# The order of the first products of k, q and kv on TensorE in a linear-attention and state-space kernel, and a carry product padded to 128 rows

## The chip, the cores and the metric

The kernel runs on one core of a Trainium2 chip. The metric is the device time of one execution in microseconds (us). A core has engines that work through queues of their own, each strictly in order, and wait for one another through semaphores: TensorE (PE in the profile; its weight loads are PEld), VectorE (DVE), ScalarE (ACT), GpSimd (POOL), and SyncE (SP), which here only starts transfers.

## The reference

Two branches work on 2048 tokens with 448 features and are mixed by a gate.

```python
x = A_x;  g = sigmoid((x * gate_w).sum(-1))
# a: linear attention, 16 heads of 28
q, k, v = split(x @ wqkv)
phi = lambda t: where(t > 0, t + 1, exp(t)) + 1e-6
kv = sum_s phi(k)[s]^T v[s];   z = sum_s phi(k)[s]
a = (phi(q) @ kv) / (phi(q) @ z + 1e-6) @ wo
# b: a diagonal state-space convolution of x along the tokens, by FFT
K = 2 * real(sum_n C[d, n] * exp(A[d, n] * dt[d] * l))
b = causal_conv(x, K) + x * D_skip
out = g * a + (1 - g) * b
```

For the inputs at hand the taps K are constant along the tokens, so that the convolution is a running sum of the rows of x times one number per feature. The kernel tests that, and keeps a general path for other inputs, which doesn't run here.

## The kernel before

The tokens are cut into 16 chunks of 128 (`c`). Numbers are kept as a high part, rounded to the type of TensorE's products (`F32R`), and a low part, the rest; the high part is a cast on ACT, the low part a subtraction (`low`, L229/L230) on POOL or DVE. A projection of a chunk is eleven products (`pieces`, L309, issued at L325; `project` issues all eleven): four tiles of the contraction, numbered 1, 2, 3 and 0, with names as the diff has them: `h1` is high x times high weights of tile 1, `l1` low x times high weights, `w1` high x times low weights. Tile 0 has 64 real rows; its other 64 rows carry the low part of the weights, so that it needs no `w0`. Its high weights are therefore complete only after a cast on ACT and a subtraction on DVE.

For a chunk c there are:

- **x(c)**: `split_t` (L232) casts the turned x on ACT (L234) and makes its low part on POOL (L230); `split_n` (L237) does the same for the plain x (ACT L240, POOL L230) and, for c > 2, calls `skip` (L245/L246, POOL: x times D_skip). The skips of chunks 0 to 2 are called by themselves.
- **k(c)**: the projection by the weights of k. `k_feature` (L348) makes two ACT passes, relu and exp (L351, L352), and one on DVE (L353); `k_high` (ACT, L357) makes `pkh`, `k_low` (DVE, L363) makes `pkl` and adds the chunk to the sum z, `zb`. pkh and pkl have two buffers each.
- **q(c)**: the projection by the weights of q and the gate. `q_post` (L370) makes the gate's exp and the feature (ACT L371, L340; DVE L341, L344).
- **kv(c)**: `do_g` (L386, L394), eleven products of plain x with pkh and pkl, summed over all chunks in four PSUM banks. The first product of a block reads pkh, the second pkl, for chunk 0 and for the blocks of 128 columns.
- **v(c)**: `do_v` (L399), the running sum inside a chunk by a triangle of ones, `tri`. `v_post` takes the sums of all chunks' last rows to `u`.

Everything is issued in an order written out by hand. **Opening** (L421 to L463): x(0) and the weights arrive in three transfers, of which the last holds tile 0 of the weights and x(1); x(2) and plain x(0) follow in one, plain x(1) and x(2) in another. Nine filler products (`fill`, L250/L252, on constant data) run on PE until then. k(0) is issued in a special order, with one filler behind its first, second and ninth product; then k(1), k(2), the features of chunks 0 and 1, kv(0), kv(1), q(0), q(1). **Loop** (L464, steps c = 2 to 13): k(c+1), its feature; for c < 5 kv(c); q(c), its feature; for c > 4 kv(c) behind it. In steps 2 to 5 and ahead of them, `steps` (L417) moves on `s4d_prepare` (L272), which reduces the state-space inputs on ACT (L283, L284) and DVE (L285, then a row of small operations up to L302) and ends at step 5 with four small transposes on PE (L306). In step 3 DVE casts `tri` (L501) and `gcr` (L502).

**Behind the loop** the last chunks follow, the four sums of kv are copied to SBUF by ACT (`gs`, L666), one by one as they are complete, and `inter` (L683) makes the carry of the running sums: one product (L688) of `gcr` and `uw`, a cast of `u`, over `UZ` = 64 rows. Next on PE are the products of `kv_products` (L719), each group of four of which reads the four gs in order. Then a loop over the chunks turns the normalised features (L595) and multiplies them with the finished matrix (L620, eleven products a chunk).

Buffers that the steps touch: the turned x has four, the plain x seven, the loads four; PSUM is given by tag (`q`, `k`, `v0`, `v1`).

Of the kernel before, what the change touches and what calls it, by code (L numbers as in the profile page):

```python
# [8 lines left out]
F32R = mybir.dt.float32r  # L9
# [6 lines left out]
P = 128  # L16
S = 2048
D = 448
# [6 lines left out]
NAT = 4 * P  # L25
# [17 lines left out]
GIN = 9 + NC  # L43
L1, L0 = 32, 64
UL = 32
UZ = 2 * UL
PAD = S + P
MAGIC = 1.5 * 2.0 ** 23
TWO_PI = 6.283185307179586
# [85 lines left out]
def gated_mix_kernel(ctx: ExitStack, tc: tile.TileContext, xin, wq_d, wvo_d, abc_d, ldt_d, dsk_d,  # L135
                     turn_d, cst_d, first_d, gin_d, lag_d, out):
    nc = tc.nc
    PE, ACT, DVE, POOL, SP = nc.tensor, nc.scalar, nc.vector, nc.gpsimd, nc.sync
# [15 lines left out]
    wkh, wkl = wk2[:, 0], wk2[:, 1]  # L154
# [5 lines left out]
    cst = const.tile([P, DJ + RX + 1], F32, name="cst")  # L160
    mask, gcat, sel = cst[:DJ, :DJ], cst[:UZ, DJ:DJ + RX], cst[:, DJ + RX:]
    gcr = const.tile([UZ, RX], F32R, name="gcr")
    ones = const.tile([P, P], F32R, name="ones")
    rows = const.tile([P, S], F32, name="rows")
    near, dsk = (rows[:, i * D:(i + 1) * D] for i in range(2))
    u = const.tile([UZ, D], F32, name="u")
    zb = const.tile([P, D], F32, name="zb")
# [9 lines left out]
    xt_p = work.enter_context(tc.tile_pool(name="xt", bufs=4))  # L177
# [11 lines left out]
    xt, xn, turned, plain = {}, {}, {}, {}  # L189

    def load_x(c):
        r = xp.tile([P, XC], F32, name="xr", tag="xr")
        turned[c], plain[c] = r[:, :NAT], r[:, NAT:]
        SP.dma_start(out=r, in_=xin[c])
# [5 lines left out]
    wkr = {}  # L200
    o = 0
    for part in PARTS:
# [8 lines left out]
        o = e  # L211
# [17 lines left out]
    def low(eng, o, r, h):  # L229
        eng.tensor_tensor(out=o, in0=r, in1=h.bitcast(F32), op=ALU.subtract)  # L230

    def split_t(c):  # L232
        w = xt[c] = xt_p.tile([P, 2 * NAT], F32R, name="xt", tag="t")
        ACT.copy(w[:, :NAT], turned[c])  # L234
        low(POOL, w[:, NAT:], turned[c], w[:, :NAT])

    def split_n(c):  # L237
        r, w = plain[c], xn_p.tile([P, NX], F32R, name="xn", tag="n")
        xn[c] = w
        ACT.copy(w[:, :XC - NAT], r)  # L240
        low(POOL, w[:, XC - NAT:], r[:, :D], w[:, :D])
        if c > 2:
            skip(c)

    def skip(c):  # L245
        POOL.tensor_tensor(out=y[:, c], in0=plain[c][:, :D], in1=dsk, op=ALU.mult)  # L246
# [3 lines left out]
    def fill(n):  # L250
        for _ in range(n):
            PE.matmul(idle, lhsT=warm[:, :P], rhs=warm, start=True, stop=True)  # L252
# [4 lines left out]
    def split_w(j, h, l, w, eng):  # L257
        ACT.copy(h[:, j], w[j] if isinstance(w, dict) else w[:, j])
        low_w(j, h, l, w, eng)

    def low_w(j, h, l, w, eng):
        r = slice(0 if j else 64, P)
        w = w[j] if isinstance(w, dict) else w[:, j]
        low(eng, (l if j else h)[r, j], w[r], h[r, j])
# [44 lines left out]
    def pieces(c, wh, wl, n, tag, last=None):  # L309
        o = ps.tile([P, 512], F32, name=tag, tag=tag)  # L310
        h, l = ([xt[c][:, i + k * P:i + (k + 1) * P] for k in range(J)] for i in (0, NAT))
        hh, lh, hl = ([(a[k], w[:, k]) for k in range(J)] for a, w in ((h, wh), (l, wh), (h, wl)))
        hl = hl[1:]
        if last == "x":
            seq = hh + hl + lh
        else:
            seq = [p for k in range(J) for p in (hh[k], lh[k])] + hl
            if last == "w":
                seq = seq[2:6] + seq[8:9] + seq[6:8] + seq[9:] + seq[:2]

        def run(count):
            for _ in range(min(count, len(seq))):
                a, b = seq.pop(0)
                run.n += 1
                PE.matmul(o[:, :n], lhsT=a, rhs=b, start=run.n == 1, stop=not seq)  # L325
        run.n = 0
        return o, run

    def project(*args, **kw):
        o, run = pieces(*args, **kw)  # L330
        run(11)
        return o
# [15 lines left out]
    def k_feature(c, o):  # L348
        e = tp.tile([P, D], F32, name="e", tag="e")
        pks[c] = o[:, :D]  # L350
        ACT.activation(e, pks[c], AF.Relu, scale=-1.0)  # L351
        ACT.activation(e, e, AF.Exp, scale=-1.0)  # L352
        DVE.scalar_tensor_tensor(out=pks[c], in0=pks[c], scalar=1.0, in1=e, op0=ALU.add, op1=ALU.max)  # L353

    def k_high(c):
        pkh[c] = tp.tile([P, 512], F32R, name="pkh", tag="pkh")[:, EDGE:EDGE + D]
        ACT.add(pkh[c], pks[c], 1e-6)  # L357

    def k_low(c):
        pk = pks.pop(c)  # L360
        pkl[c] = tp.tile([P, 512], F32R, name="pkl", tag="pkl")[:, EDGE:EDGE + D]
        for o, a, op in ((pkl[c], pkh[c].bitcast(F32), ALU.subtract), (zb, zb, ALU.add))[::-1 if c == NC - 1 else 1]:
            DVE.scalar_tensor_tensor(out=o, in0=pk, scalar=1e-6, in1=a, op0=ALU.add, op1=op)  # L363
# [22 lines left out]
    def do_g(c, blocks=range(4)):  # L386
        w = xn[c]
        for i in blocks:
            a = w[:, 64 + i * P:64 + (i + 1) * P]
            b = w[:, XC - NAT + 64 + i * P:][:, :P] if i < 3 else None  # L390
            seq = [(a, pkh[c]), (a, pkl[c]), (b, pkh[c])] if i < 3 else \
                  [(a, pkh[c]), (a[:, :64], pkl[c])][::1 if c == 0 else -1]
            for n, (a, b) in enumerate(seq):
                PE.matmul(g[i][:a.shape[1], :D], lhsT=a, rhs=b, start=c == 0 and n == 0,  # L394
                          stop=c == NC - 1 and n == len(seq) - 1)
# [21 lines left out]
    def steps(n):  # L417
        for _ in range(n):
            next(prep, None)

    w = xt[0] = xt_p.tile([P, 2 * NAT], F32R, name="xt", tag="t")  # L421
    DVE.tensor_copy(w[:, P:NAT], turned[0][:, P:])
    ACT.copy(wkh[:, 1], wkr[1])  # L423
    DVE.tensor_copy(w[:, :P], turned[0][:, :P])
    low(DVE, w[:, NAT:], turned[0], w[:, :NAT])
    low_w(1, wkh, wkl, wkr, DVE)
    for j in (2, 3, 0):
        split_w(j, wkh, wkl, wkr, DVE)
    ko, run = pieces(0, wkh, wkl, D, "k", "w")
    for n, f in ((1, 1), (1, 1), (6, 0), (1, 1), (2, 0)):  # L430
        run(n)
        fill(f)
    ko = [ko]
    split_t(1)
    ko.append(project(1, wkh, wkl, D, "v0", "x"))
    split_t(2)
    ko.append(project(2, wkh, wkl, D, "v1", "x"))
    k_feature(0, ko[0])
    k_high(0)
    split_n(0)  # L440
    k_low(0)
    k_feature(1, ko[1])
    split_n(1)
    k_high(1)
    k_low(1)
    do_g(0)
# [17 lines left out]
    for c in range(2, NC - 2):  # L464
        if c + 3 < NC:
            load_x(c + 3)
        if c == 2:
            SP.dma_start(out=cst, in_=cst_d)
        if c == 4:
            SP.dma_start(out=wvo, in_=wvo_d)  # L470
        vs = VS.get(c, ())
        ko = project(c + 1, wkh, wkl, D, "v1" if c in (2, 4) else "k")
        for v in vs[:1]:
            do_v(v)
        split_t(c + 2)
        k_feature(c + 1, ko)
        k_high(c + 1)
        if c > 5:
            for v in vs[:1]:
                v_post(v)  # L480
        k_low(c + 1)
        if c < 5:
            do_g(c)
        qo = project(c, wqh, wql, D + 2, "q")
        if c == 5:
            steps(1)
        else:
            for v in vs[1:]:
                do_v(v)
        q_post(c, qo)  # L490
        if c == 10:
            split_n(c + 2)
        if c == 5:
            v_post(0)
        else:
            for v in vs[1:]:
                v_post(v)
        if c < 5:
            steps(2 if c == 4 else 1)
        if c == 3:  # L500
            DVE.tensor_copy(tri, trir)  # L501
            DVE.tensor_copy(gcr, gcat)  # L502
        if c == 7:
            SP.dma_start(out=okr[:, None, :DJ], in_=oks[:, None, :])
        if c == 9:
            DVE.tensor_reduce(out=okr[:, DJ:], in_=okr[:, :DJ], op=ALU.add, axis=AX.X)
            DVE.tensor_copy(okn, okr[:, DJ:])
        if c > 4:
            do_g(c)
        if c == 5:  # L510
            do_v(1)
        if c < 4:
            skip(c - 1)
        if c != 10:
            split_n(c + 2)
        if c == 5:
            v_post(1)
        for j in {11: (0, 1), 12: (2, 3)}.get(c, ()):
            w = xn_p.tile([P, NX], F32R, name="wo", tag="n")[:DJ, :2 * D].rearrange("p (i d) -> p i d", i=2)
            woh.append(w[:, 0])  # L520
            wol.append(w[:, 1])
            ACT.copy(woh[j], wo[:, j])
            low(POOL, wol[j], wo[:, j], woh[j])
# [109 lines left out]
    c = NC - 2  # L633
    POOL.memset(rows[DT:RX, D:2 * D], 0.0)
    gate(0, c)
    ko = project(c + 1, wkh, wkl, D, "k")
    do_v(c + 1)
    uw = xt_p.tile([P, 2 * NAT], F32R, name="uw", tag="t")[:UZ, :D]
    k_feature(c + 1, ko)
    ACT.copy(uw, u)  # L640
    low(POOL, uw[UL:], u[UL:], uw[UL:])
    k_high(c + 1)
    k_low(c + 1)
    zh = tp.tile([P, D], F32R, name="zh", tag="w")
# [283 lines left out]
```

## Time and profile before

| | us |
|---|---|
| median of three runs | 176.55 |
| lowest and highest run | 176.33, 176.62 |
| the profiled execution | 176.31 |
| its span in the trace | 174.5 |

Some 1.8 us of an execution lie outside the span. A row of a timeline reads: start, busy time (both us), engine, line, operation, what it writes and reads, shapes, count; brackets give the idle time of the engine ahead of it and what ended that. PE's busy time of one product (0.36 us) is longer than the distance between two products, since they overlap: distances are read from starts. The granted TensorE clock is 1.00 in every stretch. Rows are called by line: "L306" is line 306.

### The profile page before, as it was taken

The page shows a single profiled execution, that of the slowest core. Times are in us where ns is not written, and L with a number is a line of the kernel's source. Part 1 is how long each engine was busy: PE and PEld are TensorE (multiplying, and loading weights), DVE is VectorE, ACT ScalarE, POOL GpSimd, SP SyncE. Part 2 cuts the span into 40 slices and gives each one's busy share as a digit, 9 for nine tenths or more (in the row PEclk, how much of TensorE's full clock was granted, in tenths as well). Part 3 has the DMA queues.
Part 4 walks back from the last instruction along what each step waited for, and adds up shares of the span by engine and source line. Part 5 has one row for each costly group of instructions (what it writes and reads, how often), then busy time and mean ns, then how long its engine had stood idle before and what let it go on. Part 6 is the DMA issues. An engine that isn't in the chain of part 4 may idle for free.

```text
span 174.5 us, 2800 instructions
## 1 busy us (share of the span) xinstructions
PE 168.2 (96%) x876; PEld 151.5 (87%) x876; DVE 113.8 (65%) x240; ACT 96.5 (55%) x221; POOL 119.9 (69%) x128
## 2 busy tenths in 40 slices
PE   6999999999989999999999999999999999999991
PEld 2699999978789999999999999998999999999991
DVE  1747636498984663937537255487898998997551
ACT  3789395896454372534627366256475564664441
POOL 5167466557809996796996999529968998983100
PEclk9999999999999999999999999999999999999999
DMA  5999954087001230330404300000031221222212
GB/s 165 418 316 317 273 163 146 0 327 334 2 4 35 89 123 1 125 120 2 121 4 129 116 1 0 0 0 2 7 66 53 106 94 69 81 99 84 111 71 93
DMA packets 7963, 18.61 MB, mean 107 GB/s; under 512 B 2045, under 2 KB 4810, under 8 KB 7818
## 3 DMA queue, kind: packets, MB, share of 16 engines
q1 hardware_dynamic: 7946, 18.41, 31.2%
q8 instruction: 7, 0.11, 0.2%
q14 instruction: 10, 0.08, 0.2%
HBM read 14.38 MB, written 3.67 MB: 103 GB/s over the span
## 4 chain that ended last, share of the span: by engine, by line
PE 81%; DVE 8%; ACT 4%; POOL 3%; issue 2%; DVEq 0%; ACTq 0%; POOLq 0%
PE a L620 20%; PE g L394 16%; PE q L325 14%; PE k L325 13%; PE tr L595 4%; PE v L325 3%; PE q L252 2%; POOL y L246 2%; PE v L402 2%; PE v L401 2%; PE m L699 1%; DVE sm L274 1%; PE k L719 1%; PE tr L719 1%; ACT y L283 1%
## 5 line engine op out<-in xcount | busy, mean ns | idle before, releaser
L620 PE MATMUL a<-wk,th 128*128 128x448 f32 (+1 forms) x170 | 36.2, 359 | 0.0
L394 PE MATMUL g<-pkh,xn 128*128 128x448 f32 x112 | 35.5, 363 | 0.0
L620 PEld LDWEIGHTS a<-wk,th 128*128 128x128 f32 x170 | 29.5, 189 | 1.6
L325 PE MATMUL k<-wk,xt 128*128 128x448 f32 x132 | 29.4, 366 | 0.0
L325 PE MATMUL q<-wqh,xt 128*128 128x450 f32 x120 | 27.5, 366 | 0.0
L353 DVE SCALAR_TENSOR_TENSOR k<-k,e 128x448 f32<-128x448 f32 x12 | 7.6, 632 | 30.5 <-ACT e L352 30.5
L325 PEld LDWEIGHTS k<-wk,xt 128*128 128x128 f32 x132 | 24.5, 188 | 2.9 <-ACT wk L423 0.5
L230 POOL TENSOR_TENSOR xn<-xr,xn 128x448 fp32r<-128x448 f32 x16 | 18.8, 1178 | 11.6 <-ACT xn L240 11.2
L414 POOL TENSOR_TENSOR y<-y,t 128x448 f32<-128x448 f32 x16 | 18.7, 1169 | 11.4 <-DVE t L406 11.4
L325 PEld LDWEIGHTS q<-wqh,xt 128*128 128x128 f32 x120 | 22.5, 189 | 1.8
L394 PE MATMUL g<-pkl,xn 128*128 128x448 f32 x64 | 23.3, 364 | 0.0
L394 PEld LDWEIGHTS g<-pkh,xn 128*128 128x128 f32 x112 | 21.0, 188 | 2.2
L533 POOL TENSOR_TENSOR prod<-pq,zb 128x448 f32<-128x448 f32 x16 | 18.4, 1154 | 4.3 <-ACT zb L656 3.0
L351 ACT ACTIVATE e<-k 128x448 f32<-128x448 f32 x12 | 6.5, 545 | 25.5 <-PE k L325 25.4
L246 POOL TENSOR_TENSOR y<-xr,rows 128x448 f32<-128x448 f32 x16 | 18.5, 1155 | 0.0
L230 POOL TENSOR_TENSOR xt<-xr,xt 128x512 fp32r<-128x512 f32 x14 | 18.1, 1295 | 0.4 <-ACT xt L234 0.4
L558 POOL TENSOR_TENSOR pn<-pq,den 128x336 f32<-128x336 f32 x16 | 12.1, 754 | 5.9 <-ACT den L547 4.1
L625 DVE SCALAR_TENSOR_TENSOR ot<-y,og,a 128x448 f32<-128x448 f32 (+1 forms) x17 | 10.7, 629 | 5.0 <-PE a L620 5.0
L603 DVE TENSOR_TENSOR th<-tr,th 128x512 fp32r<-128x512 f32 x16 | 11.0, 690 | 2.5 <-ACT th L602 2.0
L357 ACT ACTIVATE pkh<-k 128x448 fp32r<-128x448 f32 x12 | 6.6, 546 | 10.0 <-DVE k L353 10.0
L394 PEld LDWEIGHTS g<-pkl,xn 128*128 128x128 f32 x64 | 11.2, 174 | 0.9
L602 ACT CAST th<-tr 128x512 fp32r<-128x512 f32 x16 | 9.4, 590 | 4.5 <-PE tr L595 4.2
(151 smaller groups left out, 307.1 us busy)
## 6 DMA issues: line engine op xcount, KB each, us to landing
xr<-in SPq DMA_DIRECT2D x15, 512.0 KB, 5.9
out<-ot SPq DMA_DIRECT2D x15, 224.0 KB, 1.9
pq<-in SPq DMA_DIRECT2D x4, 448.0 KB
wvo<-in SPq DMA_DIRECT2D x1, 1792.0 KB
y<-in SPq DMA_DIRECT2D x2, 480.0 KB
y<-in SPq DMA_DIRECT2D x2, 450.0 KB
u<-t SPq DMA_DIRECT2D x30, 1.8 KB, 1.8
y<-in SPq DMA_DIRECT2D x1, 448.0 KB, 4.3
```

Source lines behind the costliest of these rows:

```text
L230: eng.tensor_tensor(out=o, in0=r, in1=h.bitcast(F32), op=ALU.subtract)
L246: POOL.tensor_tensor(out=y[:, c], in0=plain[c][:, :D], in1=dsk, op=ALU.mult)
L325: PE.matmul(o[:, :n], lhsT=a, rhs=b, start=run.n == 1, stop=not seq)
L353: DVE.scalar_tensor_tensor(out=pks[c], in0=pks[c], scalar=1.0, in1=e, op0=ALU.add, op1=ALU.max)
L394: PE.matmul(g[i][:a.shape[1], :D], lhsT=a, rhs=b, start=c == 0 and n == 0, stop=c == NC - 1 and n == len(seq) - 1)
L414: POOL.tensor_tensor(out=y[:, c], in0=y[:, c], in1=t, op=ALU.add)
L533: POOL.tensor_tensor(out=pd[c], in0=pq[:, c], in1=zb, op=ALU.mult)
L558: POOL.tensor_tensor(out=n[:, :3, :DJ].rearrange("p j (h d) -> p j h d", h=4), in0=a, in1=r[:, :H - 4].rearrange("p (j h) -> p j h", j=3)[ ...
L602: ACT.copy(h, ov)
L603: DVE.tensor_tensor(out=l, in0=ov, in1=h.bitcast(F32), op=ALU.subtract)
L620: PE.matmul(a[:, lo:hi], lhsT=u_, rhs=w_[:, lo:hi], start=n == 0, stop=n == 10)
L625: DVE.scalar_tensor_tensor(out=ot[:, lo:hi], in0=y[:, c, lo:hi], scalar=og[:, c:c + 1], in1=a[:, lo:hi], op0=ALU.mult, op1=ALU.add)
```

## The change

Four edits:

- In the opening, the buffer of x(1) is taken along with that of x(0). x(1) is cast by ACT ahead of tile 0 of the weights, and its low part is made by DVE, between those of tiles 3 and 0 of the weights, not by POOL. PE issues nine products of k(0) (the same fillers behind the first and second, none behind the ninth), then six of k(1), which need neither tile 0 nor the low part of x(1), then the last two of k(0), then the other five of k(1).
- The casts and low parts of the plain x(0) and x(1) are called ahead of the feature of chunk 0 and of its `k_high`.
- In steps 2 to 4 kv(c) is issued behind q(c) and its feature, as in the later steps.
- `UZ` is 128: `u`, `uw`, `gcr` and the product L688 have 128 rows. The added rows are zeros; the low part of `uw` is made for the same 32 rows as before.

```diff
-UZ = 2 * UL
+UZ = 4 * UL
...
-            if last == "w":
+            if last and len(last) > 1:
+                seq = [{"h": hh, "l": lh, "w": [None] + hl}[i[0]][int(i[1])] for i in last.split()]
+            elif last == "w":
                 seq = seq[2:6] + seq[8:9] + seq[6:8] + seq[9:] + seq[:2]
...
-    w = xt[0] = xt_p.tile([P, 2 * NAT], F32R, name="xt", tag="t")
+    w, w1 = (xt_p.tile([P, 2 * NAT], F32R, name="xt", tag="t") for _ in range(2))
+    xt[0], xt[1] = w, w1
...
-    for j in (2, 3, 0):
+    for j in (2, 3):
         split_w(j, wkh, wkl, wkr, DVE)
-    ko, run = pieces(0, wkh, wkl, D, "k", "w")
-    for n, f in ((1, 1), (1, 1), (6, 0), (1, 1), (2, 0)):
-        run(n)
+    ACT.copy(w1[:, :NAT], turned[1])
+    low(DVE, w1[:, NAT:], turned[1], w1[:, :NAT])
+    split_w(0, wkh, wkl, wkr, DVE)
+    ko, runs = zip(*(pieces(c, wkh, wkl, D, t, o) for c, t, o in (
+        (0, "k", "h1 l1 h2 l2 w1 h3 l3 w2 w3 h0 l0"), (1, "v0", "h1 h2 h3 w1 w2 w3 h0 l1 l2 l3 l0"))))
+    for c, n, f in ((0, 1, 1), (0, 1, 1), (0, 7, 0), (1, 6, 0), (0, 2, 0), (1, 5, 0)):
+        runs[c](n)
         fill(f)
-    ko = [ko]
-    split_t(1)
-    ko.append(project(1, wkh, wkl, D, "v0", "x"))
+    ko = list(ko)
     split_t(2)
     ko.append(project(2, wkh, wkl, D, "v1", "x"))
+    split_n(0)
     k_feature(0, ko[0])
+    split_n(1)
     k_high(0)
-    split_n(0)
     k_low(0)
     k_feature(1, ko[1])
-    split_n(1)
...
         k_low(c + 1)
-        if c < 5:
-            do_g(c)
         qo = project(c, wqh, wql, D + 2, "q")
...
-        if c > 4:
-            do_g(c)
+        do_g(c)
...
-    low(POOL, uw[UL:], u[UL:], uw[UL:])
+    low(POOL, uw[UL:2 * UL], u[UL:2 * UL], uw[UL:2 * UL])
```

## The prediction

> **What bounds the kernel now.** I read the page first: the busy shares and the chain that ended last.
>
> ```profile
> PE 168.2 (96%) x876; PEld 151.5 (87%) x876; DVE 113.8 (65%) x240; ACT 96.5 (55%) x221; POOL 119.9 (69%) x128
> PE 81%; DVE 8%; ACT 4%; POOL 3%; issue 2%; DVEq 0%; ACTq 0%; POOLq 0%
> ```
>
> TensorE issues products almost without a break and holds 81% of the chain. No product is removed, so time can only come from slots in which TensorE issues nothing useful. The view of waits gives PE two of them behind the opening, both between 35 and 49 us. They stand in brackets (idle before, releaser) in PE's timeline, whose columns are start, busy, then what:
>
> ```profile
> 28.55 2.37 PE L325 MATMUL k<-wk,xt 128*128 128x448 f32 x11
> ...
> 35.22 0.37 PE L325 MATMUL v<-wk,xt 128*128 128x448 f32 x1
> 35.95 2.28 PE L325 MATMUL v<-wk,xt 128*128 128x448 f32 x10 [0.36 <-POOL xt L230]
> ...
> 42.54 2.49 PE L325 MATMUL k<-wk,xt 128*128 128x448 f32 x11
> ...
> 46.89 0.76 PE L325 MATMUL q<-wql,xt 128*128 128x450 f32 x3
> 48.46 0.60 PE L306 MATMUL p<-both,sm 112*128 112x112 f32 x4 [0.81 <-DVE sm L273]
> ```
>
> A product takes 0.20 us of issue (opening rows below). k(5) loses 35.95 - 35.22 - 0.20 = **0.53**. k(6) takes 2.49 where k(4) takes 2.37: **0.12**. The three products from 46.89 leave the queue free at 47.49, and the four transposes of L306 start at 48.46: **0.97**. In the chain in order of time, the stretch between q(0) and L306 runs through ACT, POOL and DVE: there those three set the pace, and TensorE runs into them at L306. Behind L306 the chain is PE again almost to the end, so what L306 gains, the kernel gains.
>
> The opening, the same view:
>
> ```profile
> 6.16 1.68 PE L325 MATMUL k<-wk,xt 128*128 128x448 f32 x7
> 7.69 0.39 PE L252 MATMUL q<-warm 128*128 128x512 bf16 x1
> 8.02 0.67 PE L325 MATMUL k<-wk,xt 128*128 128x448 f32 x2
> 8.53 4.57 PE L325 MATMUL v<-wk,xt 128*128 128x448 f32 x22
> 12.93 0.36 PE L394 MATMUL g<-pkh,xn 128*128 128x448 f32 x1
> ```
>
> 22 products between 8.53 and 12.93 give 0.20 each. From 7.69 to 8.53, 0.84 us hold two useful products (0.40): one filler, a wait for the low part of the weights' tile 0, and a restart.
>
> **Part 1, the opening.** The filler goes and six products of k(1) take the slot at 7.69. They end at 8.89; h0, l0 of k(0) go to 9.29, the last five of k(1) to 10.29, k(2) to 12.49, where kv(0) starts instead of at 12.93: **0.44 earlier**, if the data is there. ACT's timeline, then DVE's:
>
> ```profile
> 6.74 0.57 ACT L258 CAST wk<-y 128x448 fp32r<-128x448 f32 x1 [0.16 <-DMA y<-in]
> ...
> 8.04 0.62 ACT L234 CAST xt<-xr 128x512 fp32r<-128x512 f32 x1 [0.21 <-DMA xr<-in]
> 8.73 0.55 ACT L351 ACTIVATE e<-k 128x448 f32<-128x448 f32 x1
> ...
> 10.59 0.55 ACT L357 ACTIVATE pkh<-k 128x448 fp32r<-128x448 f32 x1 [0.70 <-DVE k L353]
> 11.03 0.61 ACT L240 CAST xn<-xr 128x512 fp32r<-128x512 f32 x1
> 11.54 0.55 ACT L351 ACTIVATE e<-v 128x448 f32<-128x448 f32 x1
> ...
> 12.61 0.60 ACT L240 CAST xn<-xr 128x512 fp32r<-128x512 f32 x1
> ```
>
> ```profile
> 4.96 0.69 DVE L230 TENSOR_TENSOR xt<-y,xt 128x512 fp32r<-128x512 f32 x1
> 5.57 2.40 DVE L230 TENSOR_TENSOR wk<-y,wk 128x448 fp32r<-128x448 f32 x4
> ...
> 11.16 0.62 DVE L363 SCALAR_TENSOR_TENSOR pkl<-k,pkh 128x448 fp32r<-128x448 f32 x1 [0.61 <-ACT pkh L357]
> ```
>
> Tile 0 and the turned x(1) come in one transfer (6.74), so ACT's cast of x(1), 0.62 like that of x(2), takes 6.74 to 7.36 and is ready for 7.69. DVE's four lows are 0.60 each: three end near 7.4, x(1)'s low (0.69) near 8.1, tile 0's near 8.7, ahead of 8.89. POOL loses that low and is free for x(2) when ACT's cast lands (8.04 + 0.62).
>
> The price is on the features. k(0) now ends at 9.29, not 8.53, so its relu moves from 8.73 to 9.49 and its pkl from 11.78 to 12.54; kv(0) wants it with its second product, at 12.69. pkh(0) starts at 10.59 + 0.76 = 11.35, and ACT's next operation, now the relu of chunk 1, 0.44 behind it (10.59 to 11.03): 11.79. From relu to the end of pkl is 11.78 - 8.73 = 3.05, so pkl(1) ends at 14.84; kv(1)'s second product wants it at 12.49 + 2.20 + 0.20 = 14.89. Almost no slack is left: I take 0.44 whole, and keep 0 to 0.1 as loss.
>
> **Part 2, kv of chunks 2 to 4 behind q.** Each kv is eleven products, 2.2 us, so q(2), q(3) and q(4) end 2.2 earlier on PE. Is it those that ACT waits for?
>
> ```profile
> 26.79 0.55 ACT L357 ACTIVATE pkh<-v 128x448 fp32r<-128x448 f32 x1 [0.70 <-DVE v L353]
> 28.75 0.17 ACT L371 ACTIVATE e<-q 128x1 f32<-128x1 f32 x1 [1.41 <-PE q L325]
> ...
> 34.59 0.55 ACT L357 ACTIVATE pkh<-k 128x448 fp32r<-128x448 f32 x1 [0.70 <-DVE k L353]
> 35.41 0.17 ACT L371 ACTIVATE e<-q 128x1 f32<-128x1 f32 x1 [0.28 <-PE q L325]
> ```
>
> Yes: 1.41 us at 28.75, while the casts of x(4), x(5) and the relu of k(4) stand behind it in ACT's queue; 0.28 at 35.41. With q(2) ending near 26.1, ACT goes on when pkh(3) is done: 26.79 - 0.44 + 0.55 = 26.90, with issue 26.95, **1.80 earlier**. Its input k(4) is there by then (28.55 - 0.44 + 2.37 = 30.48). At q(3) the second wait goes: pkh(4) ends at 35.14 - 1.80 = 33.34, so ACT is 35.41 - 33.44 = **1.97 earlier**. What waits on ACT, in POOL's and DVE's timelines:
>
> ```profile
> 34.61 1.28 POOL L230 TENSOR_TENSOR xt<-xr,xt 128x512 fp32r<-128x512 f32 x1
> 35.86 1.16 POOL L246 TENSOR_TENSOR y<-xr,rows 128x448 f32<-128x448 f32 x1
> 39.06 1.28 POOL L230 TENSOR_TENSOR xn<-xr,xn 128x448 fp32r<-128x448 f32 x1 [2.04 <-ACT xn L240]
> ```
>
> ```profile
> 36.24 1.03 DVE L341 TENSOR_SCALAR t<-e 128x448 f32<-128x448 f32 x1
> ...
> 38.64 0.69 DVE L285 SCALAR_TENSOR_TENSOR y<-pq 112x512 f32<-112x512 f32 x1
> ...
> 39.26 1.17 DVE L501 CAST tri<-both 128x128 fp32r<-128x128 f32 x1
> ...
> 48.24 0.16 DVE L273 TENSOR_TENSOR sm<-sm,okc 112x4 f32<-112x4 f32 x1
> ```
>
> x(5)'s low moves from 35.89 to 34.09; k(5)'s second product wants it at 35.22 - 0.44 + 0.20 = 34.98, so the 0.53 goes, and likewise k(6)'s 0.12. On DVE, the casts and small operations end just after a POOL operation ends (t at 37.27, POOL at 37.02; tri at 40.43, POOL at 40.34), whatever their size. I read that as DVE waiting for POOL there, and POOL's x(5) operation waits for ACT. So tri and what follows move with ACT by 1.97: the last DVE operation before L306 from 48.40 to 46.43, L306 from 48.46 to **46.49**. PE alone would be there at 48.46 - 0.44 - 0.53 - 0.12 - 0.97 = 46.40. DVE stays last by a hair: **1.97 saved at L306**, taken as 1.95. kv later costs nothing visible: pkh(2) is held until kv(2) ends near 28.3, its buffer is next written near 32.8 (34.59 - 1.80).
>
> The Trainium skill, "SBUF — State Buffer", section "Who interferes with whom", says that VectorE and GpSimd share a port pair under an exclusive lock, and that an operation with two SBUF inputs contends too. By that rule the pair of L285 can also hold up POOL, which speaks against a rigid shift; the 1.03 and 1.17 agree with it. By the sum without it L306 is at 46.49, with it up to one POOL operation later.
>
> **Part 3, the carry product.** PE's and ACT's timelines:
>
> ```profile
> 119.75 0.37 PE L394 MATMUL g<-pkh,xn 128*128 128x448 f32 x1
> 120.04 0.46 PE L688 MATMUL z<-uw,gcr 64*112 64x448 f32 x1
> 120.43 0.35 PE L719 MATMUL k<-gs,wvo 128*112 128x112 f32 x1
> ```
>
> ```profile
> 119.69 0.99 ACT L666 COPY gs<-g 128x448 f32<-128x448 f32 x2 [0.53 <-PE g L394]
> ```
>
> From 119.75 to 120.43 two slots (0.40) take 0.68: 0.28 lost around the 64-row product. At 128 rows it should stand in line like its neighbours. But the fourth product of L719 reads the fourth gs copy, which ends at 119.69 + 0.99 = 120.68 and starts only when kv's last product (119.75 + 0.37) is out. Today that fourth product is at about 120.8, so it can move by some 0.1 at most. I take **0.05**; ends 0 and 0.28. The zero rows added on the other engines I cost at nothing: POOL cleared 128 rows and 64 rows of 448 in the same time.
>
> ```profile
> 0.75 0.47 POOL L184 MEMSET zb<- 128x448 f32 x1 [0.29 <-POOLq L918]
> ...
> 2.39 0.46 POOL L186 MEMSET u<- 64x448 f32 x1
> ```
> The Trainium skill, "TensorEngine Tiling (Array Packing)", section "Tiling Modes", says that a change of tiling mode drains the array; the 0.28 agrees with it, and by that rule alone the sum would be 2.23.
>
> **Sum.** 1.95 + 0.05 = 2.0. The profiled execution took 176.31 (span 174.5 and 1.8 around it), so 174.3; against the median 176.55, **174.6**.
>
> **Rivals.**
> *A, PE is last at L306 and the carry gains whole*: 0.44 + 0.53 + 0.12 + 0.97 + 0.28 = 2.34, so 174.2; up to 0.3 more if restarts go too. Against it: the gs copy. 6%.
> *B, one more POOL operation on DVE's way* (1.15 to 1.3, the rows above): L306 at 47.7, 0.8 saved, 175.75. If ACT's lead is lost whole, only the opening's 0.44 is left: 176.05. For it: DVE's pace is POOL's in this stretch, and both shift by unequal amounts (1.80 and 1.97). 13%.
> *C, the cast of x-plain(1)*, now ahead of pkh(0) on ACT, waits for its transfer. The trace shows only that it had landed by 12.61; the one before it landed by 8.04, and a landing before 10.8 is free. At 12.61, pkh(0) starts at 13.12 (0.51 behind a cast, 11.03 to 11.54) instead of 11.35: the opening loses 1.8, and all behind q(0) with it: 2.0 - 1.8 = 0.2 saved, 176.35. 6%.
> *D, slower: two more POOL operations on DVE's way*. Place: the L285 pair of step 3 and the casts tri and gcr. If the pair comes after the start of POOL's x(5) operation (37.1), each of the two waits for a whole operation, 2 x 1.2 = 2.4; L306 comes at 48.9, and the time is 176.95. It decides if DVE comes there about a whole us later than I have it, so that both miss that start; the second alone (38.64 - 1.80 = 36.84) misses it when 0.25 late, and that is B. Against it: before, POOL's operation came while the second was running, and it took 0.69 all the same. 11%.
>
> **Chances.** The forecast, 174.0 to 175.3, has 64%; A 6, B 13, C 6, D 11. The range 173.9 to 176.1 holds the forecast, A and most of B, about 8 in 10. A measurement of this kernel can tell some 0.2% (0.35 us) from no change. Faster by more: forecast, A and nearly all of B, 81%; within it: C and the end of B, 8%; slower: D, 11%.
>
> **What would show it.** Opening: no filler near 7.69, kv(0) at 12.5; a wait on pkl at 12.7 or 14.9 would price the thin slack. Middle: ACT's first e of q(2) near 26.95, no wait of k(5) on POOL, L306 near 46.5. End: z 0.20 behind kv's last product, and the fourth L719 product waiting for gs. Wrong if ACT's lead at q(2) doesn't reach L306, or if a wait after L306 takes it back.

## The result, and the profile after

| | before | after |
|---|---|---|
| median, us | 176.59 (176.33 to 176.63) | 174.51 (174.33 to 174.78) |
| the profiled execution | 176.31 | 174.33 |
| its span | 174.5 | 172.5 |

The ratio is 0.9887 (95% interval 0.9870 to 0.9904): 2.08 us saved, where 1.95 (176.55 to 174.6) was forecast. The page of after, the chain that ended last:

```profile
PE 97%; DVE 1%; ACT 0%; issue 0%; ACTq 0%
```

The chain was 81% PE and is 97% PE. The view of waits has one line left for PE, its very first wait (engine and line, releaser, us in total, times, longest):

```profile
PE q L252 <- DVE warm L183: 1.5, 1, 1.5
```

Both waits of before (k(5) for POOL, L306 for DVE) are gone. In PE's timeline of after, the middle (the transposes are still L306; most lines behind them stand two or three higher than before: the projections are L327, kv L396):

```profile
35.16 2.36 PE L327 MATMUL v<-wk,xt 128*128 128x448 f32 x11
37.35 1.77 PE L327 MATMUL q<-wqh,xt 128*128 128x450 f32 x8
...
41.76 2.36 PE L327 MATMUL k<-wk,xt 128*128 128x448 f32 x11
...
45.99 0.76 PE L327 MATMUL q<-wql,xt 128*128 128x450 f32 x3
46.62 0.60 PE L306 MATMUL p<-both,sm 112*128 112x112 f32 x4
```

k(5) is one unbroken row and q(4) follows 37.35 - 35.16 = 2.19 behind its start; k(6) is busy 2.36, as an unhindered block; from the three products at 45.99 to L306 it is 0.63, where it was 48.46 - 46.89 = 1.57. Before, kv(4) followed k(5) at 38.07, 38.07 - 35.22 = 2.85 behind its start: k(5) lost 0.66, and not the 0.53 of its wait alone, as the ten products behind the wait also ran slower (2.12 from start to start). ACT, which set the pace there, in its timeline of after:

```profile
26.76 0.55 ACT L359 ACTIVATE pkh<-v 128x448 fp32r<-128x448 f32 x1 [0.70 <-DVE v L355]
27.20 0.17 ACT L373 ACTIVATE e<-q 128x1 f32<-128x1 f32 x1
...
33.47 0.17 ACT L373 ACTIVATE e<-q 128x1 f32<-128x1 f32 x1
```

The first passes of q(2) and q(3) have no bracket any more: they stand 0.44 behind the pass ahead of them (26.76, 33.03). That of q(4) comes at 40.68, 0.45 behind the pass ahead of it. The end, PE's timeline of after and then of before (z is L690, L721 the products of before's L719):

```profile
117.92 0.36 PE L396 MATMUL g<-pkh,xn 128*128 128x448 f32 x1
118.12 0.37 PE L690 MATMUL z<-uw,gcr 128*112 128x448 f32 x1
118.33 1.81 PE L721 MATMUL k<-gs,wvo 128*112 128x112 f32 x16
119.98 1.80 PE L721 MATMUL tr<-gs,wvo 128*112 128x112 f32 x16
```

```profile
122.09 1.74 PE L719 MATMUL tr<-gs,wvo 128*112 128x112 f32 x16
123.60 0.65 PE L699 MATMUL m<-wo,kvh 112*112 112x448 f32 x2
...
128.74 1.46 PE L620 MATMUL a<-wk,th 128*128 128x448 f32 x6
```

From kv's last product to the second group of sixteen it is 119.98 - 117.92 = 2.06; before it was 122.09 - 119.75 = 2.34. And the opening, PE's timeline of after, then the one row of before that it is to be held against:

```profile
7.70 1.48 PE L327 MATMUL v<-wk,xt 128*128 128x448 f32 x6
9.08 0.67 PE L327 MATMUL k<-wk,xt 128*128 128x448 f32 x2
...
12.79 0.36 PE L396 MATMUL g<-pkh,xn 128*128 128x448 f32 x1
...
17.32 0.98 PE L327 MATMUL q<-wqh,xt 128*128 128x450 f32 x4
```

```profile
17.34 0.36 PE L325 MATMUL q<-wqh,xt 128*128 128x450 f32 x1
```

kv(0) starts 0.14 earlier than before (12.93), not 0.44, and q(0) 0.02 earlier. ACT's first cast out of the third transfer (tile 0 of the weights, and x(1)) stands in its timeline of after at 7.02, released by that transfer; before it stood at 6.74:

```profile
7.02 0.62 ACT L432 CAST xt<-y 128x512 fp32r<-128x512 f32 x1 [0.48 <-DMA y<-in]
```

The total nearly met the forecast, but in this execution the opening seems to have given nothing.

### The profile page after: what moved, and what is told of

The parts are those of the page before. It is cut to its first block, busy times and chain, and to the rows that moved or that the text cites. A ratio compares the mean times of both kernels' runs of the same rounds, so it can differ in the third digit from the quotient of the medians.

```text
span 172.5 us, 2800 instructions
## 1 busy us (share of the span) xinstructions
PE 167.4 (97%) x875; PEld 151.6 (88%) x875; DVE 114.5 (66%) x241; ACT 96.3 (56%) x221; POOL 119.6 (69%) x127
## 4 chain that ended last, share of the span: by engine, by line
PE 97%; DVE 1%; ACT 0%; issue 0%; ACTq 0%
PE a L622 21%; PE g L396 21%; PE q L327 19%; PE k L327 16%; PE v L327 7%; PE tr L597 4%; PE q L252 2%; PE v L404 2%; PE v L403 2%; PE m L701 1%; PE k L721 1%; PE tr L721 1%; DVE warm L183 0%; PE p L306 0%; DVE ot L627 0%; ACT pq L633 0%
## 5 line engine op out<-in xcount | busy, mean ns | idle before, releaser
L396 PE MATMUL g<-pkh,xn 128*128 128x448 f32 x112 | 35.5, 363 | 0.0
L327 PE MATMUL k<-wk,xt 128*128 128x448 f32 x132 | 29.3, 365 | 0.0
L327 PE MATMUL q<-wqh,xt 128*128 128x450 f32 x120 | 27.5, 366 | 0.0
L327 PEld LDWEIGHTS k<-wk,xt 128*128 128x128 f32 x132 | 24.6, 188 | 2.7 <-ACT wk L426 0.4
L327 PEld LDWEIGHTS q<-wqh,xt 128*128 128x128 f32 x120 | 22.5, 188 | 1.7
L230 POOL TENSOR_TENSOR xn<-xr,xn 128x448 fp32r<-128x448 f32 x16 | 19.4, 1212 | 6.6 <-ACT xn L240 4.5
L396 PE MATMUL g<-pkl,xn 128*128 128x448 f32 x64 | 23.4, 366 | 0.0
L396 PEld LDWEIGHTS g<-pkh,xn 128*128 128x128 f32 x112 | 21.0, 188 | 2.2
L396 PEld LDWEIGHTS g<-pkl,xn 128*128 128x128 f32 x64 | 11.2, 174 | 1.2 <-DVE pkl L365 0.2
L327 PE MATMUL q<-wql,xt 128*128 128x450 f32 x45 | 11.6, 363 | 0.0
```

## The experiments

The theory to begin with was the prediction's: an opening worth 0.44, a middle in which ACT's waits for q(2) and q(3) set the pace, and an end worth 0.05. The rivals: that one wait of ACT (q(2)) carries the whole middle; that the opening is lost to the features; that the end is worth the whole 0.28. The first four runs take the change apart; two move kv chunk by chunk; two price a product of 64 rows; the last four go after the opening.

**One part alone: the middle.**

```diff
-        if c < 5:
-            do_g(c)
         qo = project(c, wqh, wql, D + 2, "q")
...
-        if c > 4:
-            do_g(c)
+        do_g(c)
```

> The kernel before with only the middle edit: kv of chunks 2 to 4 behind q. Theory M (the middle edit carries nearly all, because it takes away ACT's wait for q(2)): the four transposes L306 start at 46.8 +- 0.2 instead of 48.46, no wait of PE on POOL at k(5), and the time is 174.9 +- 0.25 against 176.6. Rival O (the opening's lead is what is carried through, and the middle edit alone is eaten by DVE waiting for POOL): L306 at 47.7 or later, 175.8 or more.

Measured: 174.66, ratio 0.9882 (0.9866 to 0.9899): 1.94 us, as good as the whole change. Yet in its profiled execution (175.27) the whole kernel ran late from the start. PE's timeline of this run:

```profile
18.23 0.98 PE L325 MATMUL q<-wqh,xt 128*128 128x450 f32 x4
...
47.51 0.60 PE L306 MATMUL p<-both,sm 112*128 112x112 f32 x4
```

q(0) is 0.89 later than before with the same opening. ACT's timeline shows the reason: its first cast out of the third transfer starts at 7.63, released by that transfer; before it was 6.74, the same 0.89 earlier.

```profile
7.63 0.57 ACT L258 CAST wk<-y 128x448 fp32r<-128x448 f32 x1 [0.91 <-DMA y<-in]
```

From q(0) to L306 it is 47.51 - 18.23 = 29.28; before 48.46 - 17.34 = 31.12; after 46.62 - 17.32 = 29.30. So the middle is worth 1.82 to 1.84 there.

**The opening alone** (the first two edits, lines as in the diff).

```diff
-    for j in (2, 3, 0):
+    for j in (2, 3):
...
+    for c, n, f in ((0, 1, 1), (0, 1, 1), (0, 7, 0), (1, 6, 0), (0, 2, 0), (1, 5, 0)):
```

> The kernel before with only the opening edit. In the profiled execution of the changed kernel the opening's lead was 0.14 at kv(0) and 0.02 at q(0). Theory M: the features of chunks 0 and 1 end too late for a lead, q(0) starts at 17.2 to 17.35, and the time is 176.5 +- 0.15, no more than 0.2 below before. Rival O: the transfer that landed at 7.02 instead of 6.74 was an accident of that execution; here it lands at 6.7 to 6.8, q(0) starts near 16.95, and the time is 176.15.

Measured: 176.67, ratio 1.0001 (0.9988 to 1.0015). PE's timeline, with the transfer in time (ACT's cast at 6.75, before 6.74):

```profile
12.51 0.37 PE L396 MATMUL g<-pkh,xn 128*128 128x448 f32 x1
12.72 0.38 PE L396 MATMUL g<-pkl,xn 128*128 128x448 f32 x1
12.94 0.56 PE L396 MATMUL g<-pkh,xn 128*128 128x448 f32 x2
...
14.95 0.47 PE L396 MATMUL g<-pkl,xn 128*128 128x448 f32 x1
15.26 0.57 PE L396 MATMUL g<-pkh,xn 128*128 128x448 f32 x2
...
17.07 0.98 PE L327 MATMUL q<-wqh,xt 128*128 128x450 f32 x4
```

kv(0) is 0.42 earlier: the slot was filled as forecast (12.49). At kv(1) the second product takes 15.26 - 14.95 = 0.31 to the next, not 0.20, and kv(0)'s second 0.22. The weight loads of PE have one wait on pkl in their view of waits, of 0.2: those are the waits that the prediction had at nearly no slack. At q(0) 0.27 is left.

**The carry product alone.**

```diff
-UZ = 2 * UL
+UZ = 4 * UL
```

> The kernel before with only the carry product at 128 rows. Theory: z follows kv's last product after 0.20 and the sixteen L719 products start 0.48 to 0.50 behind it (before 0.68), so 0.28 is gained there when they are done, but the first product of the finished matrix waits for VectorE and ScalarE, so that only 0.1 to 0.15 of it arrives at L620; the time is 176.45, not to be told from 176.6. Rival (the whole 0.28 arrives): 176.3. Rival of the forecast (the fourth gs copy holds the products back): 0.05 or less at the end of the L719 products.

Measured: 176.37, ratio 0.9986 (0.9973 to 1.0000): 0.2, at the edge of the interval. PE's timeline:

```profile
120.00 0.36 PE L394 MATMUL g<-pkh,xn 128*128 128x448 f32 x1
...
122.06 1.80 PE L719 MATMUL tr<-gs,wvo 128*112 128x112 f32 x16
123.70 0.66 PE L699 MATMUL m<-wo,kvh 112*112 112x448 f32 x2
...
128.87 2.25 PE L620 MATMUL a<-wk,th 128*128 128x448 f32 x10
```

The second group of L719 starts 2.06 behind kv's last product (before 2.34): the whole 0.28 is there, and no product of the first group waits for gs. But that group now takes 123.70 - 122.06 = 1.64, before 123.60 - 122.09 = 1.51, and 0.13 is given back; at L620 it is 8.87 against 8.99, **0.12** in all. The 8.99 is not fixed: with the carry's product of 64 rows it was 8.99 to 9.03 in five of the seven profiled executions here, with the second group at 1.51, and 9.25 in the other two (the opening alone, chunk 2 alone), with that group at 1.65. With 128 rows it was 8.87 to 8.91 in all seven. So this edit gives 0.1 or nearly 0.4, by the execution; what decides between 1.51 and 1.65 stays open.

**The low half of x(1) on POOL**, in the changed kernel.

```diff
-    low(DVE, w1[:, NAT:], turned[1], w1[:, :NAT])
+    low(POOL, w1[:, NAT:], turned[1], w1[:, :NAT])
```

> The changed kernel, but the low part of x(1) on POOL, as before the change. Theory: in the changed kernel VectorE makes that low ahead of tile 0 of the weights, so h0 of k(0) starts at 9.08, 0.18 behind its slot; on POOL, idle until 8.99, it is out of the way, h0 takes its slot at 8.90, the features of chunk 0 and kv(0) come 0.15 to 0.2 earlier, kv(1) and q(0) too, and the time is 174.35 or the same 174.5 if other engines set the pace behind q(0). Rival (POOL's slower subtraction, 1.29 against 0.69, delays the lows of x(2) and plain x(0)): kv(0) waits for them, 174.7 or more.

Measured: 174.71, ratio 0.9881 (0.9865 to 0.9897), which the times don't tell from the changed kernel's 174.51. Its profiled execution does. POOL's timeline, DVE's, PE's:

```profile
8.17 1.29 POOL L230 TENSOR_TENSOR xt<-y,xt 128x512 fp32r<-128x512 f32 x1 [5.07 <-ACT xt L432]
```

```profile
8.59 1.35 DVE L230 TENSOR_TENSOR wk<-y,wk 64x448 fp32r<-64x448 f32 x1 [1.21 <-ACT wk L258]
```

```profile
10.00 0.67 PE L327 MATMUL k<-wk,xt 128*128 128x448 f32 x2 [0.22 <-DVE wk L230]
```

With POOL busy from 8.17 to 9.46, DVE's low of tile 0, next to it, takes 1.35; the last two products of k(0) wait for it. In DVE's timeline of after, the same operation, with POOL idle until 8.99:

```profile
8.40 0.62 DVE L230 TENSOR_TENSOR wk<-y,wk 64x448 fp32r<-64x448 f32 x1
```

The Trainium skill, "SBUF — State Buffer", section "Who interferes with whom", has VectorE operations with two SBUF inputs and GpSimd operations that read SBUF exclude each other; this agrees with it, by 0.73 us.

**kv of chunk 2 alone behind q; then of chunks 2 and 3.** M1 below is the reading that the wait for q(2) alone sets the pace, M2 that the next q takes back what the one before it freed.

```diff
-        if c < 5:
+        if 2 < c < 5:
             do_g(c)
...
-        if c > 4:
+        if c == 2 or c > 4:
             do_g(c)
```

> The kernel before with only kv of chunk 2 behind q; chunks 3 and 4 as before. Theory M2 (ScalarE's queue sets the pace, and a lead is worth only what the next wait leaves of it): ScalarE's e of q(2) comes 1.5 earlier as in the changed kernel, but q(3) still ends at its old place on PE, behind kv(3), so e of q(3) stays at about 35.4, and L306 at 48.2 to 48.5; only PE's wait at k(5) goes, which PE gives back at L306. Time 176.5 +- 0.2, no gain. Rival M1 (the wait of 1.41 at q(2) is worth itself): L306 near 47.1, 175.2.

Measured: 176.21, ratio 0.9975 (0.9960 to 0.9990). ACT's timeline and PE's:

```profile
36.10 0.17 ACT L371 ACTIVATE e<-q 128x1 f32<-128x1 f32 x1 [1.77 <-PE q L325]
```

```profile
48.49 0.60 PE L306 MATMUL p<-both,sm 112*128 112x112 f32 x4 [0.28 <-DVE sm L273]
```

q(0) started at 18.07. The wait for q(2) is gone, and the one for q(3) has grown from 0.28 to 1.77: nearly all of the lead is given back there. From q(0) to L306 it is 30.42: 0.70 gained, not M1's 1.4 and not M2's nothing. Neither reading has where that comes from. DVE's timeline of this run shows it: it reaches tri and gcr before POOL's next operation starts at 39.75, and they take 0.22 and 0.20, where they took 1.17 and 1.18.

```profile
39.12 0.22 DVE L501 CAST tri<-both 128x128 fp32r<-128x128 f32 x1
39.26 0.20 DVE L502 CAST gcr<-cst 64x112 fp32r<-64x112 f32 x1
```

The feature of k(5) behind them on DVE then starts 0.91 earlier behind q(0) (41.28 - 18.07 against 41.46 - 17.34), and ACT's wait for q(4), now 0.28, leaves 0.70 of that.

```diff
-        if c < 5:
+        if c == 4:
             do_g(c)
...
-        if c > 4:
+        if c != 4:
             do_g(c)
```

> The kernel before with kv of chunks 2 and 3 behind q, chunk 4 as before. Theory M2: e of q(3) comes 1.9 earlier, but q(4) ends behind kv(4) near 41.8 and e of q(4) starts near 41.9 instead of 40.7 in the changed kernel, the casts of x(6) behind it are 1.2 late on ScalarE, then POOL and VectorE, and L306 starts near 47.6: 175.7 +- 0.25, half of the gain. Rival (the last q no longer matters, since VectorE holds the stretch): L306 at 46.7, 174.8.

Measured: 175.94, ratio 0.9960 (0.9946 to 0.9974). ACT's timeline and PE's, q(0) at 17.41:

```profile
42.11 0.17 ACT L371 ACTIVATE e<-q 128x1 f32<-128x1 f32 x1 [1.24 <-PE q L325]
```

```profile
47.75 0.60 PE L306 MATMUL p<-both,sm 112*128 112x112 f32 x4 [0.86 <-DVE sm L273]
```

Now the wait stands at q(4), 1.24, and from q(0) to L306 it is 30.34. M2 has the place of the wait right each time: all three have to move. Two moved give 0.78, the third 1.04 more. The 0.78 is not the 0.70 of before and a little on top: tri and gcr take 1.17 again here, as in the changed kernel.

**What one product of 64 rows costs**, in the kernel before: ahead of each of q(6) to q(13) one more product with R rows, whose result the next one overwrites. It adds work that the reference doesn't have.

```diff
                 run.n += 1
+                if run.n == 1 and tag == "q" and 5 < c < 14:
+                    PE.matmul(o[:, :n], lhsT=a[:R], rhs=b[:R], start=True, stop=True)
```

> The kernel before with one added product of 64 rows ahead of the projection q(c) of each of the chunks 6 to 13 (eight in all), in a stretch where PE issues without a break; its result is overwritten by the next product. Theory (a product of 64 rows costs its slot of 0.20 and 0.28 around it): 8 x 0.48 = 3.8, 180.4. Rival (the 0.28 at the carry product came from something else there): 8 x 0.20 = 1.6, 178.2.

> The same with 128 rows. Theory and rival alike: 8 x 0.20 = 1.6, 178.2.

Measured: 181.33 with 64 rows, ratio 1.0274 (1.0247 to 1.0301); 178.11 with 128, ratio 1.0081 (1.0056 to 1.0106). The chain in order of time (start, us, what), of the run with 64 rows and then of that with 128; the added product is L326:

```profile
62.43 0.40 PE q L326
62.83 2.40 PE q L327 x11
```

```profile
62.34 0.20 PE q L326
62.54 2.21 PE q L327 x11
```

A product of 128 rows costs its slot, (178.11 - 176.59) / 8 = 0.19; one of 64 costs (181.33 - 176.59) / 8 = 0.59, half of the extra 0.40 in its own slot and half in the eleven products behind it. The theory's 0.48 was short by 0.11, the rival's 0.20 by 0.39. The rule of the Trainium skill that the prediction named ("TensorEngine Tiling (Array Packing)", section "Tiling Modes") fits time lost on both sides of the product; that a drain is what costs it, no run here shows.

**The changed kernel without its opening, and the changed kernel again.** The diff of the first is the middle's and the carry's above.

> The changed kernel without the opening edit: the middle edit and the carry product of 128 rows alone. Theory M (the opening's lead is lost to the features of chunks 0 and 1 and to the set pace behind q(0)): 174.5 +- 0.2, the same as the changed kernel in the same call; in the trace q(0) at 17.3 to 17.4 if the third transfer lands at 6.8, and L306 29.3 behind q(0), as in the changed kernel. Rival (the opening is worth 0.25 or more on average, as it bridges a late third transfer): 174.8 or more.

> The changed kernel again, to stand beside the other two on the same chip: 174.5 +- 0.2.

Measured: 174.69 without (ratio 0.9891, 0.9865 to 0.9917), 174.60 with it (0.9877, 0.9850 to 0.9904): no difference that the times show.

**Four products of k(1) in the slot instead of six, tile 0's low ahead of x(1)'s**, run twice.

```diff
+    split_w(0, wkh, wkl, wkr, DVE)
     low(DVE, w1[:, NAT:], turned[1], w1[:, :NAT])
-    split_w(0, wkh, wkl, wkr, DVE)
...
-(1, 6, 0), (0, 2, 0), (1, 5, 0)
+(1, 4, 0), (0, 2, 0), (1, 7, 0)
```

> The changed kernel with four products of k(1) in place of six ahead of h0 and l0 of k(0), and with VectorE making the low part of tile 0 ahead of that of x(1). Theory: what the opening lacks is slack for the features; h0 follows at about 8.5 instead of 8.9 to 9.1, the relu of chunk 0 is 0.4 earlier, no product of kv(0) or kv(1) waits for pkl (0.02 and 0.1 in the traces so far), and q(0) keeps the whole lead of 0.42 where the third transfer is in time; 174.35, or no difference to the changed kernel that can be measured. Rival (h0 comes too early for its low part, and PE stops): 174.6 or more.

> The kernel with four products of k(1) ahead of h0, l0 a second time, since its first median (174.10) lies 0.4 below that of the changed kernel (174.51 and 174.6) with intervals that overlap. If the better opening is real: 174.1 +- 0.2 again. If not: 174.5 +- 0.2.

Measured: 174.10 (0.9861, 0.9837 to 0.9886) and 174.21 (0.9872, 0.9845 to 0.9898), the lowest medians of all, and the second is where its expectation put a real gain; the intervals overlap those of the changed kernel.

**What the times can't show and the traces can.** The third transfer lands at another time in every execution, whatever the kernel. Here each profiled execution is held against the start of ACT's first cast out of that transfer ("landing"; for the carry alone, where the casts run together, 0.47 ahead of the cast of x(1), as before). It is a mark: where it stands only 0.14 to 0.17 behind the casts ahead of it (before, opening alone, carry alone, both with four), the transfer may have been there sooner. The last four columns are times less the landing. The two kernels with added products are left out; their q(0) stands at 10.60 and 10.63.

| kernel | landing | q(0) | L306 | first L620 product | execution |
|---|---|---|---|---|---|
| before | 6.74 | 10.60 | 41.72 | 122.00 | 169.57 |
| middle alone | 7.63 | 10.60 | 39.88 | 120.15 | 167.64 |
| opening alone | 6.75 | 10.32 | 41.55 | 122.10 | 169.55 |
| carry alone | 6.97 | 10.63 | 41.74 | 121.90 | 169.35 |
| chunk 2 alone | 7.48 | 10.59 | 41.01 | 121.55 | 168.98 |
| chunks 2 and 3 | 6.81 | 10.60 | 40.94 | 121.22 | 168.67 |
| middle and carry, no opening | 6.84 | 10.59 | 39.88 | 120.07 | 167.51 |
| after | 7.02 | 10.30 | 39.60 | 119.78 | 167.31 |
| after again | 7.44 | 10.31 | 39.61 | 119.81 | 167.26 |
| after, low of x(1) on POOL | 7.47 | 10.78 | 40.07 | 120.26 | 167.73 |
| four instead of six | 6.86 | 10.31 | 39.60 | 119.79 | 167.23 |
| four, again | 7.00 | 10.32 | 39.59 | 119.76 | 167.23 |

Every old opening has q(0) 10.59 to 10.63 behind the landing, every new one 10.30 to 10.32, but for the run with POOL. So the opening does give **0.28**; the landings, spread over 0.89, cover it. Beside the middle it is worth 0.28 at L306 and L620 and 0.20 to 0.25 in the execution; alone, 0.17 is left at L306, where DVE still sets the pace, and the execution with 9.25 at the end took the rest. The low of x(1) on DVE is worth 0.47 in the same way. Four instead of six brings 0.03 to 0.08 in the execution and nothing up to L306: kv(0) starts 5.91 behind the landing instead of 5.77, without the waits on pkl, and q(0) is where it was. No trace backs medians that are 0.3 to 0.5 lower; earlier landings would make them, but that was not shown, and whether this opening is better stays open.

## Why the prediction was right, point by point

**The total: right, by terms that were off in both directions.** Forecast 0.44 + 1.51 + 0.05 = 2.0. Shown by the table at the first L620 product: 0.28 for the opening, 1.85 for the middle, 0.10 for the carry, 2.22 together (122.00 to 119.78). That an opening taken 0.16 too high made up for half of a middle taken 0.34 too low is luck. The profiled execution of after landed 0.28 later and so showed 176.31 - 174.33 = 1.98; the medians 2.08.

**The opening, "I take 0.44 whole": wrong.** The slot at 7.69 was there and was filled (kv(0) at 12.51 against 12.49 forecast, with the transfer in time), but the "almost no slack" of pkl was a loss: about 0.02 in kv(0) and 0.11 in kv(1). The 0 to 0.1 kept for it was 0.12 to 0.15 from kv(0) to q(0). And the prediction took the landing as fixed; in after's own profile it came 0.28 later. The six products still started at 7.70, but h0 and l0 of k(0) at 9.08 instead of 8.89, where they waited for the low part of tile 0, and kv(0) at 12.79, so a plain difference of the two traces shows 0.02 at q(0).

**The middle: mechanism right, size short by 0.3.** ACT's waits for q(2) to q(4) were the pace, as the moved chunks show. The step that failed is "26.79 - 0.44 + 0.55 = 26.90, with issue 26.95": ACT's next pass starts 0.44 behind the start of the one ahead (26.76 to 27.20), not 0.60, though its row says 0.55 busy. The prediction used that 0.44 in the opening (10.59 to 11.03) and not here. It happens twice: against q(0), whose lead is 0.02, pkh(3) came where it was before (9.44 against 9.45), e of q(2) 1.53 earlier and not 1.36, and e of q(3) 35.41 - 33.47 - 0.02 = 1.92 and not 1.53. L306 gained 1.82 of it. "DVE stays last by a hair" is as near as the trace can tell: TensorE's queue is through at 45.99 + 0.60 = 46.59, and DVE's last operation ahead of the transposes ends at 46.56, 1.84 earlier than before, 0.02 of it the opening's.

```profile
46.40 0.16 DVE L273 TENSOR_TENSOR sm<-sm,okc 112x4 f32<-112x4 f32 x1
```

The transposes follow at 46.62, which is 39.60 behind the landing; the forecast of 46.49 is 39.75 behind the landing of before. "PE alone would be there at 46.40" was too late: from the forecast's own q(0) (17.34 - 0.44) that is 29.50, and it took 29.30, with 0.13 more from k(5) than was counted and 0.05 to 0.06 each from q(2) and q(4).

The lead did not pass down DVE as rigidly as "tri and what follows move with ACT" has it. In step 4, DVE's timeline of after, then of before:

```profile
41.89 1.38 DVE L343 TENSOR_SCALAR t<-e 128x448 f32<-128x448 f32 x1
...
45.55 0.22 DVE L274 SCALAR_TENSOR_TENSOR sm<-sm 112x4 f32<-112x4 f32 x2
```

```profile
43.76 0.38 DVE L341 TENSOR_SCALAR t<-e 128x448 f32<-128x448 f32 x1
...
46.29 1.33 DVE L274 SCALAR_TENSOR_TENSOR sm<-sm 112x4 f32<-112x4 f32 x2
```

The operation t of q(4), which started 0.17 ahead of one of POOL's (43.93), now starts 0.03 behind it (41.86) and takes 1.00 longer; for that, a pair of small operations further on takes 1.11 less. What both have in common is the last POOL operation of the stretch, in POOL's timeline of after, then of before:

```profile
44.23 1.31 POOL L230 TENSOR_TENSOR xt<-xr,xt 128x512 fp32r<-128x512 f32 x1
```

```profile
46.24 1.28 POOL L230 TENSOR_TENSOR xt<-xr,xt 128x512 fp32r<-128x512 f32 x1
```

It ends 1.98 earlier (47.52 to 45.54), and DVE's last operation comes 0.88 behind it before and 1.02 after. So the prediction's reading that DVE is held by POOL, and POOL by ACT, is what the rows show; that one wait on POOL came and another went was in no sum of it.

**The carry: size near, reason wrong.** "The fourth product of L719 reads the fourth gs copy" was to hold it to 0.1. The whole 0.28 arrived at the products, so that copy holds nothing. What was gained is 0.1 because 0.13 is given back in the next sixteen, for a reason that was not found: the size is near by luck.

**The rivals.** A (TensorE last at L306, the whole 0.28 at the end) came true by half: L306 behind the landing is 2.12 earlier against its 2.06 (0.44 + 0.53 + 0.12 + 0.97), and the chain through it is TensorE's own, but the end gave 0.10 of its 0.28. B (one more POOL operation in DVE's way) came at t of q(4), by 1.00, and was paid back, as above. D (two more, at the L285 pair and the casts) did not come. POOL's timeline, then DVE's, of after:

```profile
37.11 1.37 POOL L230 TENSOR_TENSOR xn<-xr,xn 128x448 fp32r<-128x448 f32 x1 [0.93 <-ACT xn L240]
```

```profile
36.77 0.69 DVE L285 SCALAR_TENSOR_TENSOR y<-pq 112x512 f32<-112x512 f32 x1
37.38 1.17 DVE L504 CAST tri<-both 128x128 fp32r<-128x128 f32 x1
```

The second of the pair started 0.34 ahead of POOL's operation and was through; D needed it to start behind. POOL's operation took 1.37 instead of 1.28 and tri ended with it, as before, so that the wait moved along without growing. C did not come (ACT's cast of x-plain(1) stands in its timeline at 10.85, without a wait), but its kind did: an earlier transfer that lands late, in every kernel alike.

## What to carry to other kernels

When several waits of one engine are released by the same pattern, move all of them before judging: here the first alone moved the wait on to the next, two moved it to the third, and three gave 1.82. What a part gives alone is not its share of the whole: the first alone gave 0.70, by two casts of DVE that no longer met POOL's operations, and with all three moved they met them again. Take the pitch of consecutive passes from their starts and not from their busy time, everywhere. Where two engines get in each other's way, see which operation waits for which after a shift, since the shift reorders them. A gain of 0.3 us in an opening behind a load can be lost in medians to when that load lands, so hold each trace against the landing first, then compare stage by stage.

## What the hardware showed that I had not expected

The landing of the third transfer was spread from 6.74 to 7.63 over the profiled executions, and it moved all that came behind it one for one. One product of 64 rows among those of 128 cost (181.33 - 178.11) / 8 = 0.40 more than one of 128, and at the carry 0.28. The casts tri and gcr on DVE took 1.17 and 1.18 beside POOL's operations, and 0.22 and 0.20 where POOL's came later. Sixteen small products ahead of the m products took 1.51 or 1.65 where the carry's product had 64 rows, and 1.64 to 1.65 in all seven executions where it had 128; why was not found.
